# Key-value sums of a memory-attention block over 128 rows and eight array tiles instead of 96 rows and four

## Chip, cores and metric

One core of a Trainium2 chip runs the kernel. The metric is device time in microseconds (us), lower is better; quoted times are medians over several executions. The span of a profile (first to last instruction) is some 1.7 us shorter than the time of the same execution. All executions quoted here were fast (none was more than 1.5% above the fastest of its kernel). Tiles named `p_...` lie in PSUM, where TensorE writes, in banks; tiles named `t_...` lie in SBUF. A cited "Trainium skill" is a set of notes on the chip, named by page title.

## The reference

Eight batches, eight heads, 576 tokens, 64 columns a head. Keys and values are condensed into 32 memory rows a head with softmax weights from `phi`; queries attend to those rows; a gated feed-forward block follows.

```python
a = exp(phi - max(phi)); a = a / (sum(a, axis=2) + 1e-9)    # axis 2: the 576 tokens
k_m = einsum('bhsm,bhsd->bhmd', a, k)                       # (8, 8, 32, 64)
v_m = einsum('bhsm,bhsd->bhmd', a, v)
attn = softmax(q @ k_m.T / 8)                               # over 32 memory rows
x = (attn @ v_m) -> (4608, 512)                             # tokens x (heads * 64)
out = (silu(x @ w_gate) * (x @ w_val)) @ w_out              # d_ff 1536
```

## The kernel before

Tokens of a head lie on 96 partitions, six to a partition. The weighted sums over tokens (`p_kv`) are products of 96 rows by 32 columns: one array tile for each of four head pairs, both heads `g` of a pair in turn, all in one PSUM bank. VectorE divides by the denominators in one product of tensors each for keys and values. `NG` = 2, `NP` = 4, `J` = 6, `P` = 96, `D` = 64, `M` = 32.

```python
def kv_sum(b, p, parts):
    w0, w1 = parts[0], parts[-1] + 1
    n = (w1 - w0) * D
    for g in range(NG):
        for j in range(J):
            for i in range(NP):
                nc.tensor.matmul(p[32*i:32*i+32, n*g:n*(g+1)],
                    lhsT=ephis[b][:, j, g, i],
                    rhs=kvs[b][:, w0:w1, 2*i+g, j*D:(j+1)*D],
                    start=(j == 0), stop=(j == J-1), tile_position=(0, 32*i))

def run_sums():                        # batches 2 to 7
    o = NG * 2 * D
    p = bank([128, o + NG], FP32, "p_kv")
    kv_denominators(b, p, o)
    kv_sum(b, p, (0, 1))
    kv_reciprocal(b, p, o)
    kvv = p[:, 0:o].rearrange("p (g w d) -> p g w d", g=NG, w=2)
    k_norm(b, kvv[:, :, 0:1, :])       # one VectorE tensor_tensor
    v_norm(b, kvv[:, :, 1, :])         # one VectorE tensor_tensor
    done(p)
    if beside:
        beside()                       # the p_u products of another weight chunk
```

Batches 0 and 1 start while loads land. Their values are summed late and straight in transposed form, and dummy products (`p_warm`) fill TensorE:

```python
def v_direct(b):
    p = bank([128, NP, M], FP32, "p_vT")
    # ... 48 products of 96 rows x 64 columns ...
    nc.vector.tensor_copy(out=kTs[b][:, 2], in_=p.rearrange("p i m -> p (i m)"))

def warm(n):
    p = bank([128, DM], FP32, "p_warm")
    for _ in range(n):
        nc.tensor.matmul(p[:, 0:128], lhsT=bones, rhs=bones, start=True, stop=True)

warm(130)
# ... keys, queries, scores of batches 0 and 1, with smaller groups of dummies ...
v_direct(0)
nc.scalar.preload_act_table_set("silu_and_others")
norm(1, 0)                             # t_A of batch 1, VectorE
norm(1, 1)
warm(24)
v_direct(1)
warm(4)
run([u_half(0, (0,), 0, 0, "av"), u_half(1, (0,), 0, 0, "av")])   # first p_u group
warm(6)
for s in range(4):
    gv_gate(0, s)                      # first gate products
```

The softmax here doesn't subtract the row's maximum and nothing guards it: scores larger than these inputs give would overflow.

## Time and profile before

| | kernel before |
|---|---|
| time | 248.39 us (248.08 to 248.61, 3 runs) |
| TensorE busy | 239.5 us, 97% of a span of 246.6 us |
| VectorE / ScalarE busy | 157.9 us / 164.5 us |
| first denominators / first scores / first gate product | 11.10 / 14.89 / 28.21 us |

TensorE is the bound from about 28 us on.

### The profile page before, as it was taken

What the parts mean: (1) busy time and instruction counts of PE and PEld (TensorE: products, weight loads), DVE (VectorE), ACT (ScalarE), POOL (GpSimd) and SP (SyncE); (2) the same over time, 40 slices, a digit from 0 to 9 for tenths busy, and PEclk for the clock granted to TensorE, in tenths of its full rate; (3) what the DMA queues carried; (4) which work ended last, traced back from release to release, by engine and by line L of the source; (5) the groups of instructions that cost most, each with busy time, mean ns of one, the idle gap of its engine ahead of it and who ended that gap; (6) DMA issues with size and microseconds to landing.
All of it is one profiled execution on the core that took longest, in us unless ns stands there. A gap on an engine that the chain in (4) does not pass through costs nothing.

```text
span 246.6 us, 6607 instructions
## 1 busy us (share of the span) xinstructions
PE 239.5 (97%) x2600; PEld 151.2 (61%) x2600; DVE 157.9 (64%) x337; ACT 164.5 (67%) x356; POOL 51.4 (21%) x81
## 2 busy tenths in 40 slices
PE   7989999999999999999999999999999999999993
PEld 7965767774544766467646665476546655467543
DVE  0045599993338688478837778479746876587420
ACT  2447889885087577966896577866995678676201
POOL 8433432000060005071305230090007000000000
PEclk9999999999999999999999999999999999999998
DMA  6999999999699975995996499489414311310143
GB/s 182 206 203 203 199 207 205 232 207 184 143 158 243 247 174 82 216 297 112 153 246 177 80 152 242 136 123 187 94 44 120 69 43 43 88 43 0 45 129 85
DMA packets 47055, 37.00 MB, mean 150 GB/s; under 512 B 15920, under 2 KB 41776, under 8 KB 47024
## 3 DMA queue, kind: packets, MB, share of 16 engines
q0 software_dynamic: 25520, 22.42, 56.1%
q1 hardware_dynamic: 20496, 13.37, 22.5%
q10 hardware_dynamic: 1008, 0.79, 1.2%
q8 instruction: 20, 0.33, 0.5%
q14 instruction: 11, 0.09, 0.1%
HBM read 42.47 MB, written 9.44 MB: 210 GB/s over the span
## 4 chain that ended last, share of the span: by engine, by line
PE 95%; DVE 1%; ACT 1%; issue 0%
PE p_oo L512 38%; PE p_g L452 19%; PE p_v L452 19%; PE p_u L409 5%; PE p_warm L619 5%; PE p_kv L206 2%; PE p_oo L544 1%; DVE t_qT L348 1%; PE p_g L379 1%; PE p_g L358 1%; PE p_v L379 1%; PE p_vT L317 1%; ACT t_E L368 1%; PE p_T L270 0%; PE p_kv L226 0%
## 5 line engine op out<-in xcount | busy, mean ns | idle before, releaser
L512 PE MATMUL p_oo<-WO,t_h 128*128 128x512 bf16 x420 | 108.7, 380 | 0.0
L468 ACT ACTIVATE t_sg<-p_g 128x288 bf16<-128x288 f32 x192 | 76.3, 414 | 31.2 <-PE p_g L452 24.2
L475 DVE TENSOR_TENSOR t_h<-t_sg,p_v 128x288 bf16<-128x288 bf16 x192 | 83.4, 452 | 18.0 <-PE p_v L452 14.1
L452 PEld LDWEIGHTS <-t_U 128*128 128x128 bf16 x768 | 74.2, 98 | 30.7 <-issue 2.5
L452 PE MATMUL p_g<-t_A,t_U 128*128 128x288 bf16 x384 | 77.5, 286 | 0.1
L452 PE MATMUL p_v<-t_A,t_U 128*128 128x288 bf16 x384 | 76.9, 286 | 0.0
L512 PEld LDWEIGHTS <-t_h 128*128 128x128 bf16 x420 | 39.5, 98 | 41.1 <-issue 6.1
L524 DVE COPY t_o<-p_oo 128x512 f32<-128x512 f32 x27 | 18.6, 690 | 31.9 <-PE p_oo L512 29.4
L433 DVE CAST t_U<-p_u 128x512 bf16<-128x512 f32 x42 | 26.7, 683 | 6.8 <-PE p_u L409 6.8
L429 ACT CAST t_U<-p_u 128x512 bf16<-128x512 f32 x30 | 15.8, 592 | 8.9 <-PE p_u L409 8.9
L522 ACT COPY t_o<-p_oo 128x512 f32<-128x512 f32 x8 | 4.7, 588 | 20.1 <-PE p_oo L512 10.6
L115 POOL DMA_DIRECT2D t_q<-in_q_dram x6 | 4.7, 779 | 60.8 <-DMA t_qT<-t_q 59.5
L619 PE MATMUL p_warm<-bones 128*128 128x128 bf16 x198 | 15.2, 239 | 1.5 <-DVE bones L635 1.5
L176 ACT ACTIVATE t_ephi<-t_phi 96x768 bf16<-96x768 f32 x16 | 12.5, 843 | 4.2 <-DMA t_phi<-in_phi_dram 4.2
L409 PE MATMUL p_u<-W,t_kT 64*32 64x512 bf16 (+1 forms) x416 | 15.2, 365 | 0.1
L619 PEld LDWEIGHTS <-bones 128*128 128x128 bf16 x198 | 13.4, 109 | 2.2 <-DVE bones L635 1.5
L189 POOL COPY t_mark<-t_A 1x1 bf16<-1x1 bf16 x4 | 0.7, 180 | 54.9 <-DVE t_A L389 54.9
L368 ACT ACTIVATE t_E<-p_g 128x288 bf16<-128x288 f32 x16 | 6.6, 412 | 8.3 <-PE p_v L358 7.8
L389 DVE TENSOR_TENSOR t_A<-t_E,t_lz 128x576 bf16<-128x576 bf16 x16 | 11.5, 750 | 0.5 <-ACT t_lz L384 0.5
L384 ACT ACTIVATE t_lz<-t_lz 128x576 f32<-128x576 f32 x16 | 10.9, 683 | 0.5
L193 POOL TENSOR_TENSOR t_es<-t_es,t_ephi 96x256 f32<-96x256 f32 x16 | 10.7, 666 | 1.3
L610 ACT ACT_TABLE_LOAD x7 | 9.0, 1283 | 1.3 <-PEq L798 1.2
(58 smaller groups left out, 159.8 us busy)
## 6 DMA issues: line engine op xcount, KB each, us to landing
t_kv<-in_k_dram POOLq DMA_DIRECT2D x8, 576.0 KB, 9.6
t_kv<-in_v_dram POOLq DMA_DIRECT2D x8, 576.0 KB, 14.3
out_dram<-t_o SPq DMA_DIRECT2D x23, 192.0 KB, 2.5
t_phi<-in_phi_dram POOLq DMA_DIRECT2D x6, 576.0 KB, 16.5
t_q<-in_q_dram POOLq DMA_DIRECT2D x6, 576.0 KB, 8.0
out_dram<-t_o SPq DMA_DIRECT2D x24, 128.0 KB, 2.4
WO<-in_moe_w_out_dram POOLq DMA_DIRECT2D x3, 512.0 KB, 19.5
out_dram<-t_o SPq DMA_DIRECT2D x23, 64.0 KB, 2.1
```

The lines of the kernel that those rows point to most:

```text
L176: nc.scalar.activation(out=t[:, :, g].rearrange("p j i m -> p i j m"), in_=src[:, g], func=AF.Exp)
L384: nc.scalar.activation(out=lz, in_=lz, func=AF.Exp, scale=-1.0)
L389: nc.vector.tensor_tensor(out=a, in0=es.pop((b, g)), in1=lzs.pop((b, g)), op=ALU.mult)
L409: nc.tensor.matmul(p[g][32 * i:32 * i + 32, o:o + n], lhsT=kTs[b][64 * g:64 * g + 64, 2, 32 * i:32 * i + 32], rhs=w_part(w, c, i, g, halve ...
L429: nc.scalar.copy(out=t, in_=p)
L433: nc.vector.tensor_copy(out=t, in_=p)
L452: nc.tensor.matmul(p[:, 0:HALF], lhsT=Us[b, c, g][:, o // 2, which, 128 * (o % 2):128 * (o % 2 + 1)], rhs=atts[b, g][:, r], start=(g == 0) ...
L468: nc.scalar.activation(out=sg, in_=gate[:, 0:HALF], func=AF.Silu)
L475: nc.vector.tensor_tensor(out=dst, in0=sg, in1=val[:, 0:HALF], op=ALU.mult)
L512: nc.tensor.matmul(mine["p"], lhsT=hts[c, jf][:, 128 * u:128 * (u + 1)], rhs=WO[jf], start=(jf == 0), stop=(jf == NJF - 1),)
L524: nc.vector.tensor_copy(out=t_o, in_=mine["p"])
L619: nc.tensor.matmul(p[:, 0:128], lhsT=bones, rhs=bones, start=True, stop=True)
```

## The change

The intent: use all 128 partitions and both row halves of the array. Head pairs are laid over 128 partitions, 64 rows a head and nine tokens a row (`JK` = 9), so that a wave of sums is eight tiles of 64 x 32, two banks. Loads get fewer and longer pieces, and the sums have the tiling of `p_u`. Batches 0 and 1 have `phi` with zeros for the other head, so that products over 128 rows serve one head. Dummies become 512 columns wide. Cut to its core:

```diff
-        t = inp.tile([P, 2, H, J * D], BF16, tag="kv", name="t_kv")
-        nc.gpsimd.dma_start(out=t[:, 0], in_=k[b].rearrange("h (p j) d -> p h (j d)", p=P))
+        t = inp.tile([128, 2, NP, JK * D], BF16, tag="kv", name="t_kv")
+        nc.gpsimd.dma_start(out=t[:, 0], in_=head_pairs(k[b]))
 ...
-        for g in range(NG):
-            for j in range(J):
-                for i in range(NP):
+        for j in range(JK):
+            for i in range(NP):
+                for g in range(NG):
                     nc.tensor.matmul(
-                        p[32 * i:32 * i + 32, n * g:n * (g + 1)],
+                        p[g][32 * i:32 * i + 32, 0:n],
 ...
-                        tile_position=(0, 32 * i),
+                        tile_position=(64 * g, 32 * i),
 ...
+    def scaled_copy(out, p, r):
+        nc.vector.tensor_scalar(out=out, in0=p, scalar1=r, scalar2=None, op0=ALU.mult)
     def k_norm(b, p):                  # v_norm likewise
-        nc.vector.tensor_tensor(out=bk, in0=p..., in1=rSs[b]..., op=ALU.mult)
+        for g in range(NG):
+            scaled_copy(bk[:, g], x, rSs[b][:, g:g + 1])
 ...
     def v_direct(b):                   # 36 products of 128 rows
-        nc.vector.tensor_copy(out=kTs[b][:, 2], in_=p.rearrange("p i m -> p (i m)"))
+        for g in range(NG):
+            for o in range(2):
+                nc.vector.tensor_copy(
+                    out=dst[64 * g:64 * g + 64, :, o], in_=p[64 * o:64 * o + 64, :, g]
+                )
 ...
-    phi_exp(0)
-    phi_exp(1)
+    for b in range(2):
+        phi_zeros(b, nc.vector)
+        phi_exp_masked(b)
 ...
-    warm(130)                          # 130 products of 128 columns
+    warm(130, 0)                       # 32 of 512 columns and one of 256
```

More of the change, by code (lines that the diff above doesn't have):

```diff
@@ L40 @@
     P, J = 96, 6
+    JK = 9
     NG = 2
@@ L81, with head_pairs, load_phi @@
     Q_SLOT = (0, 1, 0, 0, 1, 0, 1, 0)
-    def load_phi(b, *engs):
-        t = inp.tile([P, H, J * M], FP32, tag="phi", name="t_phi")
-        n = H // len(engs)
-        for i, eng in enumerate(engs):
-            eng.dma_start(
-                out=t[:, n * i:n * (i + 1)],
-                in_=phi[b, n * i:n * (i + 1)].rearrange("h (p j) m -> p h (j m)", p=P),
-            )
+    def head_pairs(x):
+        return x.rearrange("h s d -> (h s d)").rearrange("(i p f) -> p i f", i=NP, p=128)
+    def load_phi(b, eng):
+        t = inp.tile([128, NP, JK * M], FP32, tag="phi", name="t_phi")
+        eng.dma_start(out=t, in_=head_pairs(phi[b]))
         phis[b] = t
     def load_k(b):
-        t = inp.tile([P, 2, H, J * D], BF16, tag="kv", name="t_kv")
-        nc.gpsimd.dma_start(out=t[:, 0], in_=k[b].rearrange("h (p j) d -> p h (j d)", p=P))
+        t = inp.tile([128, 2, NP, JK * D], BF16, tag="kv", name="t_kv")
+        nc.gpsimd.dma_start(out=t[:, 0], in_=head_pairs(k[b]))
         kvs[b] = t
     def load_v(b):
-        nc.gpsimd.dma_start(
-            out=kvs[b][:, 1], in_=v[b].rearrange("h (p j) d -> p h (j d)", p=P)
-        )
+        nc.gpsimd.dma_start(out=kvs[b][:, 1], in_=head_pairs(v[b]))
     def load_q_group(b, g):
@@ L167 @@
     ones1 = consts.tile([128, 1], BF16, tag="ones1", name="ones1")
+    ones2 = consts.tile([128, NG], BF16, tag="ones2", name="ones2")
     ephis, rSs, bks, bvs, kTs, es, atts = {}, {}, {}, {}, {}, {}, {}
     def phi_exp(b):
-        t = att.tile([P, J, NG, NP, M], BF16, tag="ephi", name="t_ephi")
-        src = phis.pop(b).rearrange("p (i g) (j m) -> p g i j m", g=NG, m=M)
+        t = att.tile([128, JK, NP, M], BF16, tag="ephi", name="t_ephi")
+        nc.scalar.activation(
+            out=t.rearrange("p j i m -> p i j m"),
+            in_=phis.pop(b).rearrange("p i (j m) -> p i j m", m=M),
+            func=AF.Exp,
+        )
+        ephis[b] = t
@@ L175, in phi_exp, with phi_exp_masked, phi_zeros @@
+    masked = {}
+    def phi_exp_masked(b):
+        t = masked[b]
+        src = phis.pop(b).rearrange("p i (j m) -> p i j m", m=M)
         for g in range(NG):
+            rows = slice(64 * g, 64 * g + 64)
             nc.scalar.activation(
-                out=t[:, :, g].rearrange("p j i m -> p i j m"), in_=src[:, g], func=AF.Exp
+                out=t[rows, :, g].rearrange("p j i m -> p i j m"), in_=src[rows], func=AF.Exp
             )
-        ephis[b] = t
+    def phi_zeros(b, eng):
+        t = att.tile([128, JK, NG, NP, M], BF16, tag=f"mphi{b}", bufs=1, name="t_mphi")
+        for g in range(NG):
+            eng.memset(t[64 * (1 - g):64 * (1 - g) + 64, :, g], 0.0)
+        masked[b] = t
@@ L181, with phi_of @@
+    def phi_of(b, g, j, i):
+        rows = slice(64 * g, 64 * g + 64)
+        return masked[b][rows, j, g, i] if b in masked else ephis[b][rows, j, i]
     esums = {}
     def phi_sum(b):
-        e = ephis[b].rearrange("p j g i m -> p j (g i m)")
+        e = ephis[b].rearrange("p j i m -> p j (i m)")
         mark = att.tile([1, 1], BF16, tag="mark", bufs=1, name="t_mark")
         nc.gpsimd.tensor_copy(out=mark, in_=atts[b - 1, 1][0:1, 0, 0:1])
-        t = att.tile([P, NG * 128], FP32, tag="es", bufs=1, name="t_es")
@@ L191, in phi_sum @@
-        nc.gpsimd.tensor_tensor(out=t, in0=e[:, 0], in1=e[:, 1], op=ALU.add)
-        for j in range(2, J):
-            nc.gpsimd.tensor_tensor(out=t, in0=t, in1=e[:, j], op=ALU.add)
-        hl = att.tile([P, 2, NG * 128], BF16, tag="ehl", bufs=1, name="t_ehl")
-        nc.gpsimd.tensor_copy(out=hl[:, 0], in_=t)
-        nc.gpsimd.tensor_tensor(out=hl[:, 1], in0=t, in1=hl[:, 0], op=ALU.subtract)
+        t = att.tile([128, 4, 128], FP32, tag="es", bufs=1, name="t_es")
+        add = lambda o, x, y: nc.gpsimd.tensor_tensor(out=o, in0=x, in1=y, op=ALU.add)
@@ L197, in phi_sum @@
+        add(t, e[:, 0:4], e[:, 4:8])
+        add(t[:, 0:2], t[:, 0:2], t[:, 2:4])
+        add(t[:, 0], t[:, 0], t[:, 1])
+        add(t[:, 0], t[:, 0], e[:, 8])
+        hl = att.tile([128, 2, 128], BF16, tag="ehl", bufs=1, name="t_ehl")
+        nc.gpsimd.tensor_copy(out=hl[:, 0], in_=t[:, 0])
+        nc.gpsimd.tensor_tensor(out=hl[:, 1], in0=t[:, 0], in1=hl[:, 0], op=ALU.subtract)
         esums[b] = hl
@@ L202, in kv_sum @@
         n = (w1 - w0) * D
-        for g in range(NG):
-            for j in range(J):
-                for i in range(NP):
+        for j in range(JK):
+            for i in range(NP):
+                for g in range(NG):
                     nc.tensor.matmul(
-                        p[32 * i:32 * i + 32, n * g:n * (g + 1)],
-                        lhsT=ephis[b][:, j, g, i],
-                        rhs=kvs[b][:, w0:w1, 2 * i + g, j * D:(j + 1) * D],
+                        p[g][32 * i:32 * i + 32, 0:n],
+                        lhsT=phi_of(b, g, j, i),
+                        rhs=kvs[b][64 * g:64 * g + 64, w0:w1, i, j * D:(j + 1) * D],
@@ L210, in kv_sum, with kv_denominators @@
                         start=(j == 0),
-                        stop=(j == J - 1),
-                        tile_position=(0, 32 * i),
-                    )
-    def kv_denominators(b, p, o):
+                        stop=(j == JK - 1),
+                        tile_position=(64 * g, 32 * i),
+                    )
+    def kv_denominators(b, p):
+        if b in masked:
+            for g in range(NG):
+                for j in range(JK):
+                    nc.tensor.matmul(
+                        p[:, g:g + 1],
+                        lhsT=masked[b][:, j, g].rearrange("p i m -> p (i m)"),
+                        rhs=ones1,
+                        start=(j == 0),
+                        stop=(j == JK - 1),
+                    )
+            return
@@ L216, in kv_denominators @@
         if b in esums:
             hl = esums.pop(b)
-            terms = [[hl[:, t, 128 * g:128 * (g + 1)] for t in range(2)] for g in range(NG)]
+            terms = [hl[:, t] for t in range(2)]
         else:
-            terms = [
-                [ephis[b][:, j, g].rearrange("p i m -> p (i m)") for j in range(J)]
-                for g in range(NG)
-            ]
-        for g in range(NG):
-            for n, x in enumerate(terms[g]):
-                nc.tensor.matmul(
-                    p[:, o + g:o + g + 1],
-                    lhsT=x,
-                    rhs=ones1[0:P, :],
-                    start=(n == 0),
-                    stop=(n == len(terms[g]) - 1),
-                )
@@ L234, in kv_reciprocal @@
-    def kv_reciprocal(b, p, o):
-        r = att.tile([128, NG, 1, 1], FP32, tag="rS", name="t_rS")
-        nc.vector.reciprocal(
-            out=r.rearrange("p g a c -> p (g a c)"), in_=p[:, o:o + NG]
-        )
+            terms = [ephis[b][:, j].rearrange("p i m -> p (i m)") for j in range(JK)]
+        for n, x in enumerate(terms):
+            nc.tensor.matmul(p, lhsT=x, rhs=ones2, start=(n == 0), stop=(n == len(terms) - 1))
+    def kv_reciprocal(b, p):
+        r = att.tile([128, NG], FP32, tag="rS", name="t_rS")
+        nc.vector.reciprocal(out=r, in_=p)
@@ L239, in kv_reciprocal @@
         rSs[b] = r
+    def scaled_copy(out, p, r):
+        nc.vector.tensor_scalar(out=out, in0=p, scalar1=r, scalar2=None, op0=ALU.mult)
     def k_norm(b, p):
         bk = att.tile([128, NG, 2, D], BF16, tag="bk", name="t_bk")
-        nc.vector.tensor_tensor(
-            out=bk,
-            in0=p.to_broadcast([128, NG, 2, D]),
-            in1=rSs[b].to_broadcast([128, NG, 2, D]),
-            op=ALU.mult,
-        )
+        for g in range(NG):
+            x = p[g][:, 0:D].rearrange("p (a d) -> p a d", a=1).to_broadcast([128, 2, D])
+            scaled_copy(bk[:, g], x, rSs[b][:, g:g + 1])
@@ L252, in v_norm @@
         bv = att.tile([128, NG, D], BF16, tag="bv", name="t_bv")
-        nc.vector.tensor_tensor(
-            out=bv,
-            in0=p,
-            in1=rSs[b].rearrange("p g a c -> p g (a c)").to_broadcast([128, NG, D]),
-            op=ALU.mult,
-        )
+        for g in range(NG):
+            scaled_copy(bv[:, g], p[g][:, D:2 * D], rSs[b][:, g:g + 1])
         bvs[b] = bv
@@ L278, in run_sums @@
         def run_sums():
-            o = NG * 2 * D
-            p = bank([128, o + NG], FP32, "p_kv")
-            kv_denominators(b, p, o)
+            o = 2 * D
+            p = [bank([128, CH], FP32, f"p_kv{g}") for g in range(NG)]
+            kv_denominators(b, p[0][:, o:o + NG])
             kv_sum(b, p, (0, 1))
-            kv_reciprocal(b, p, o)
-            kvv = p[:, 0:o].rearrange("p (g w d) -> p g w d", g=NG, w=2)
-            k_norm(b, kvv[:, :, 0:1, :])
-            v_norm(b, kvv[:, :, 1, :])
-            done(p)
+            kv_reciprocal(b, p[0][:, o:o + NG])
+            k_norm(b, p)
+            v_norm(b, p)
+            done(*p)
             if beside:
@@ L297, in denominators @@
             p = bank([128, NG], FP32, "p_S")
-            kv_denominators(b, p, 0)
-            kv_reciprocal(b, p, 0)
+            kv_denominators(b, p)
+            kv_reciprocal(b, p)
             done(p)
         def sums():
-            p = bank([128, NG * D], FP32, "p_kv")
+            p = [bank([128, D], FP32, f"p_kv{g}") for g in range(NG)]
             kv_sum(b, p, (0,))
-            k_norm(b, p.rearrange("p (g a d) -> p g a d", g=NG, a=1))
-            done(p)
+            k_norm(b, p)
+            done(*p)
         return [denominators, sums, lambda: kv_T(b, (0,))]
     def v_direct(b):
-        p = bank([128, NP, M], FP32, "p_vT")
-        for i in range(NP):
-            for j in range(J):
-                for g in range(NG):
+        p = bank([128, NP // 2, NG, M], FP32, "p_vT")
+        for n in range(NP // 2):
+            for j in range(JK):
+                for o in range(2):
                     nc.tensor.matmul(
-                        p[64 * g:64 * g + 64, i],
-                        lhsT=kvs[b][:, 1, 2 * i + g, j * D:(j + 1) * D],
-                        rhs=ephis[b][:, j, g, i],
+                        p[64 * o:64 * o + 64, n],
+                        lhsT=kvs[b][:, 1, 2 * n + o, j * D:(j + 1) * D],
+                        rhs=masked[b][:, j, :, 2 * n + o],
                         start=(j == 0),
-                        stop=(j == J - 1),
-                        tile_position=(0, 64 * g),
-                    )
-        nc.vector.tensor_copy(out=kTs[b][:, 2], in_=p.rearrange("p i m -> p (i m)"))
+                        stop=(j == JK - 1),
+                        tile_position=(0, 64 * o),
+                    )
+        dst = kTs[b][:, 2].rearrange("p (n o m) -> p n o m", n=NP // 2, o=2)
+        for g in range(NG):
+            for o in range(2):
+                nc.vector.tensor_copy(
+                    out=dst[64 * g:64 * g + 64, :, o], in_=p[64 * o:64 * o + 64, :, g]
+                )
         done(p)
@@ L424, in u_round @@
                 src = p[g][:, 0:(w1 - w0) * n].rearrange("p (a f) -> p a f", f=HC)
-                banks.append((dst, src, p[g], rSs[b][:, g, 0] if b in scaled else None))
+                banks.append((dst, src, p[g], rSs[b][:, g:g + 1] if b in scaled else None))
         for (t, p, home, r), e in zip(banks, evac):
@@ L613, in gv_slots, with warm @@
         return [lambda s=s: gv_slot(b, s) for s in range(2 * NJF)]
-    def warm(n):
+    def warm(n, narrow=0):
         p = bank([128, DM], FP32, "p_warm")
-        for _ in range(n):
-            nc.tensor.matmul(p[:, 0:128], lhsT=bones, rhs=bones, start=True, stop=True)
+        x = bones.rearrange("p (a c) -> p a c", a=1)
+        sizes = [1] * narrow + [4] * ((n - narrow) // 4)
+        sizes += [n - sum(sizes)] if n > sum(sizes) else []
+        for a in sizes:
+            nc.tensor.matmul(
+                p[:, 0:128 * a],
+                lhsT=bones,
+                rhs=x.to_broadcast([128, a, 128]) if a > 1 else bones,
+                start=True,
+                stop=True,
+            )
         free.insert(0, held.pop(id(p))[0])
@@ L633 @@
     nc.vector.memset(ones1, 1.0)
+    nc.vector.memset(ones2, 0.0)
+    for g in range(NG):
+        nc.vector.memset(ones2[64 * g:64 * g + 64, g:g + 1], 1.0)
     for h in range(4):
```

## The prediction

> **What bounds the kernel now.** I read the page of the kernel before first, then its waits of PE, then the timelines of PE, DVE and POOL around one key-value sum, and the start.
>
> ```profile
> PE 239.5 (97%) x2600; PEld 151.2 (61%) x2600; DVE 157.9 (64%) x337; ACT 164.5 (67%) x356; POOL 51.4 (21%) x81
> ...
> PE 95%; DVE 1%; ACT 1%; issue 0%
> ```
> ```profile
> PE p_warm L619 <- DVE bones L635: 1.5, 1, 1.5
> PE p_g L379 <- ACT t_E L368: 0.4, 1, 0.4
> PE p_g L358 <- DVE t_qT L348: 0.2, 1, 0.2
> PE p_T L270 <- PE p_warm L619: 0.2, 1, 0.2
> ```
> The first fence is the busy time of the engines and the head of the chain that ended last; the second is every wait of PE (total us, times, longest). PE works 97% of the span, is 95% of the chain, and waits 2.3 us in all, every wait within the first 22 us. From about 28 us to the end, a nanosecond off PE is a nanosecond off the kernel, as long as nothing else starts to wait. Before 28 us it is different: dummy products fill PE while loads land, so PE is busy there without being the bound.
>
> The part that the change rewrites, batch 4's sums, in the timeline of PE and of DVE (start us, duration us, engine, line):
> ```profile
> 111.10 0.24 PE L226 MATMUL p_kv<-ones,t_ehl 96*128 96x1 bf16 x4
> 111.27 0.85 PE L206 MATMUL p_kv<-t_kv,t_ephi 96*32 96x128 bf16 x48
> 112.06 0.63 PE L409 MATMUL p_u<-W,t_kT 64*32 64x512 bf16 x16
> 112.62 0.60 PE L512 MATMUL p_oo<-WO,t_h 128*128 128x512 bf16 x2
> ```
> ```profile
> 112.18 0.17 DVE L236 RECIPROCAL t_rS<-p_kv 128x2 f32<-128x2 f32 x1 [0.36 <-PE p_kv L206]
> 112.39 0.42 DVE L243 TENSOR_TENSOR t_bk<-p_kv,t_rS 128x256 bf16<-128x256 f32 x1
> 112.73 0.28 DVE L253 TENSOR_TENSOR t_bv<-p_kv,t_rS 128x128 bf16<-128x128 f32 x1
> 112.93 1.28 DVE L433 CAST t_U<-p_u 128x512 bf16<-128x512 f32 x2
> ```
> Durations overlap, so I take differences of starts. The sums hold PE from 111.27 to 112.06, 0.79 us. The records of single instructions show four products (one per column tile) starting within some 10 ns, and the next four 56 ns after them: 12 waves of 56 ns are 0.67 us. The other 0.11 us appear only where the next product uses another tiling: 149 ns from the last product to the next instead of 56, so about 93 ns for the change of tiling.
>
> The start, from the timelines of PE and POOL:
> ```profile
> 23.54 0.94 PE L317 MATMUL p_vT<-t_ephi,t_kv 96*64 96x32 bf16 x48
> 24.41 1.51 PE L619 MATMUL p_warm<-bones 128*128 128x128 bf16 x24
> 25.98 0.94 PE L317 MATMUL p_vT<-t_ephi,t_kv 96*64 96x32 bf16 x48
> ```
> ```profile
> 26.10 0.74 POOL L142 DMA_DIRECT2D W<-in_moe_w_val_dram  x1 [2.58 <-DMA t_kv<-in_v_dram]
> ```
> POOL's next issue waited for the values of batch 1, landed at 25.8 by the DMA records; PE's second direct value product starts at 25.98, after 24 dummies. The dummies are tuned to the loads.
>
> **What the Trainium skill says.** "TensorE: Matmul & The Clock Gate", section "Wait — 56ns, not 53.3ns?", gives starts N/2.4 GHz + about 2.5 ns apart once warm, N/1.2 GHz cold, and a floor near 25 ns. The trace agrees: 56 ns at 128 columns, 215.8 at 512, 25.1 to 25.5 at one column, 106.7 cold (until 5.96 us). "TensorEngine Tiling (Array Packing)", "Key Properties", says that changing the tiling mode drains TensorE; the 93 ns agree. Its "Gotcha 1: PSUM Pressure" wants different banks for different row tiles, which is why the new sums take two banks where one served; the kernel before already does so in its p_u products. "DMA: Bandwidth & Descriptors", "Why small descriptors are slow", names a fixed cost per descriptor. Here it is small: the quickest DMA engine finished loads of 768 pieces of 768 B every 2.90 us, of 512 pieces of 512 B every 1.34, and of 512 pieces of 1024 B every 2.54. Per engine (a sixteenth of the pieces) that is 0.0734 ns a byte plus 4.3 ns a piece.
>
> **The change part by part.**
>
> *Sums of batches 2 to 7.* 48 products in 12 waves of four become 72 in 9 waves of eight: 3 x 56 = 0.168 us less a batch. This supposes that eight tiles stream as freely as four. Line L409 runs the same eight tiles at 256 columns at 107 ns a wave, which is the bare 256/2.4. The doubt is supply: in the 64-column sums at 17.5 us the last pairs of weight load and product come 8.3 ns apart, against 7 ns (56/8) needed here. But about 36 pairs had gone faster before that, from a filled queue; 36 + 504/8.3 = 97 pairs are on hand in the time that 72 take, so I charge nothing.
>
> *Tiling changes.* In batches 3 to 7 the sums are followed by p_u, which has the same tiling after the change: 0.093 us less in each of five.
>
> *Denominators.* Batches 4 to 7 do two products instead of four, 2 x 25 = 0.050 us each. Batches 2 and 3 do 9 instead of 12, 0.076 each.
>
> Sum on PE: 6 x 0.168 + 5 x 0.093 + 4 x 0.050 + 2 x 0.076 = 1.83 us, all on the bound.
>
> *Normalising on DVE.* Two products of tensors (0.42 and 0.28, together 0.62) become four scalings of 128 columns. L435 scalings take 743 ns at 512 columns and 478 at 256, so 345 at 128; neighbours overlap by some 86, so 4 x 345 - 3 x 86 = 1.12 us, 0.5 more. Counted from the last sum product, DVE starts the reciprocal at +0.27 and lets go of the first bank (after its value scaling) at +1.36. PE meanwhile does p_u (0.56), two p_oo (0.43 and a 0.09 tiling change), one gate (0.24), and then wants that bank at about +1.30 for p_v. With the semaphore that is a wait of about 0.1 us, in five batches 0.5 us given back. The later banks are in time by 0.2 us or more by the same count.
>
> *ACT and POOL.* One exponential of 1152 columns (about 1.18 us, from 843 ns at 768 and 0.9 ns a column in the t_E and t_lz rows) instead of two of 768 (1.6): off the path. POOL's sum for the denominators covers 512+256+128+128 columns instead of five times 256 at 666 ns, so about 1 us sooner: no wait to remove.
>
> *Loads.* A k or v load is 512 pieces of 1152 B: 32 x (4.3 + 84.6) = 2.84 us instead of 2.90. With phi, values of batch 1 land some 0.3 us sooner. No wait after 28 us is one for a load, so this counts only at the start.
>
> *The start.* Three small memsets ahead of the diagonal blocks delay the first dummy by about 0.3 us. The 130 dummies as 32 of 512 and one of 256 run at 54 ns a 128 columns instead of 55.6 when warm; with the same clock edge they end some 0.2 us sooner. Batch 0's and 1's denominators are 18 products instead of 12: +0.17 each after the rest of the pipeline. The 64-column sums are held by supply, 0.33 against 0.36 us. Key scaling is +0.19 on the path to the transpose at 12.73. So I see the middle of the start about 0.3 later. The direct value product has 18 waves instead of 24 at 32 ns (the two 64-column weight loads seem to set it): -0.18 each; the dummies between give 0.06. But its copy on DVE is four of 64 columns, some 0.64 us instead of 0.29, and PE's p_u at 27.3 waits for that. Together +0.1 us, with perhaps 0.4 either way. The zeros (four memsets on DVE between 2 and 7 us) and the masked exponentials (6.6 to 11.1 us on ACT, batch 0's half done by 9) are in time for PE at 10.9.
>
> Total: -1.83 + 0.5 + 0.1 = -1.2 us: 247.1 us.
>
> **The rivals.** (a) *Supply of instructions bounds eight tiles.* For it: 8.3 ns a pair in the 64-column sums, and 50% more pairs. Then 72 x 8.3 = 0.60 us and a batch saves 0.07 instead of 0.17; the total is about 247.8. Against it: the filled queue. (b) *The second bank and longer DVE work become waits.* One bank more is held, and DVE is already 64% busy. If the p_u copies and the products of gate and value are late too, 0.3 us a batch is lost and the whole gain goes: 248.4. Against it: the counted slack, and a DVE that idles 14 us waiting for p_v alone. (c) *The start is freed.* If phi and keys land so much sooner, or in step on all 16 engines (the last engine is now up to 1.9 us behind the first), that PE gets to p_u sooner, 0.5 us more is won: 246.3. Against it: PE there hangs on copies by DVE and exponentials by ACT, not on loads alone. (d) *DVE scalings from PSUM cost less than extrapolated*, so no wait at all: 246.6.
>
> **Range and chances.** (c) and (d) set the low end, (a) and a mild (b) the high one, and three runs of the kernel before already spread over 0.5 us. I take 246.0 to 248.2. A gain over 2% would need 5 us, more than all the time of the rewritten products; a loss over 2% would need a new wait of 1 us in every batch. So 3% faster, 96% the same, 1% slower.
>
> **What would show it right or wrong.** In the changed profile: sums of 72 products with 0.50 to 0.56 us from their first start to that of p_u (0.60 or more says rival a); no tiling gap before p_u; PE still above 96% busy; a row of PE waiting for DVE's t_bv or t_bk of 0.1 us, five times (0.3 or more says b; none says d); the first p_u within 0.4 us of 27.3 (much earlier says c). I am wrong outright if PE gains waits on loads or on p_u copies after 28 us, or if the p_oo or gate products change their spacing.

## More of the kernel before

The prediction shows the page, the waits and one batch's sums. What it does not show is the end of the start; this is the timeline of the kernel before (start us, duration us, engine, line, operation, then idle time and its releaser in brackets):

```profile
25.95 0.76 DVE L389 TENSOR_TENSOR t_A<-t_E,t_lz 128x576 bf16<-128x576 bf16 x1 [0.47 <-ACT t_lz L384]
...
26.95 0.29 DVE L325 CAST t_kT<-p_vT 128x128 bf16<-128x128 f32 x1 [0.25 <-PE p_vT L317]
...
27.30 0.41 PE L409 MATMUL p_u<-W,t_kT 64*32 64x256 bf16 x16
...
28.21 0.77 PE L452 MATMUL p_g<-t_A,t_U 128*128 128x288 bf16 x5
```

VectorE is free for 0.25 us before the one copy behind the direct value product. The copy is done at 27.24, and the 16 `p_u` products follow in one go.

## The result, and the profile after

After: 248.82 us median (248.48 to 249.47, 4 runs) beside 248.28 us (248.08 to 248.61) for the kernel before. A ratio here is the mean time of one kernel's fast runs over that of the other's of the same rounds, so not quite the ratio of the quoted medians: 1.0024, 95% interval 1.0000 to 1.0047. Later the same kernel gave 0.9998 (0.9984 to 1.0013). The time stayed; the predicted 247.1 us and its range to 248.2 us missed it.

The page of the kernel after (busy us and share of each engine; head of the chain that ended last), then the waits of its TensorE (total us, times, longest us):

```profile
PE 236.3 (96%) x2594; PEld 143.0 (58%) x2621; DVE 163.0 (66%) x364; ACT 164.1 (66%) x350; POOL 47.5 (19%) x77
...
PE 87%; DMA 4%; DVE 4%; issue 2%; ACT 2%; SPq 0%; DVEq 0%
```
```profile
PE p_oo L538 <- issue: 2.7, 17, 0.2
PE p_warm L649 <- DVE bones L672: 1.7, 1, 1.7
PE p_g L405 <- ACT t_E L394: 0.3, 1, 0.3
PE p_u L435 <- DVE t_kT L349: 0.2, 1, 0.2
```

The trace has 2621 weight loads but 2594 products, so 27 records of products are missing, and the first row of waits (17 of 0.2 us before output products) is most likely just those holes: in e1, which has records of both output products behind the sums of batch 4, there is none. Row four is real and new.

Two stretches of the trace tell where the time went. From the first denominators (`p_S`) to the first gate product the kernel after takes 17.95 us, before 17.11. From there to the last output product's start it takes 213.88 us, before 214.35. So +0.84 us at the start and -0.47 us in the middle; with +0.02 us ahead of both, the last product starts 0.39 us later.

The middle, batch 4: the timeline of TensorE and that of VectorE of the kernel after.

```profile
111.98 0.19 PE L261 MATMUL p_kv<-ones,t_ehl 128*128 128x2 bf16 x2
112.10 0.80 PE L233 MATMUL p_kv<-t_kv,t_ephi 64*32 64x128 bf16 x72
112.69 0.66 PE L435 MATMUL p_u<-W,t_kT 64*32 64x512 bf16 x16
113.51 0.38 PE L538 MATMUL p_oo<-WO,t_h 128*128 128x512 bf16 x1 [0.16 <-issue]
113.72 0.41 PE L478 MATMUL p_g<-t_A,t_U 128*128 128x288 bf16 x2
114.15 0.42 PE L478 MATMUL p_v<-t_A,t_U 128*128 128x288 bf16 x2
```
```profile
113.09 0.17 DVE L265 RECIPROCAL t_rS<-p_kv 128x2 f32<-128x2 f32 x1 [0.38 <-PE p_u L435]
113.29 0.61 DVE L269 TENSOR_SCALAR t_bk<-p_kv,t_rS 128x128 bf16<-128x128 f32 x2
113.82 0.47 DVE L269 TENSOR_SCALAR t_bv<-p_kv,t_rS 128x64 bf16<-128x64 f32 x2
114.20 1.28 DVE L459 CAST t_U<-p_u 128x512 bf16<-128x512 f32 x2
```

The sums now hold TensorE for 0.59 us (112.10 to 112.69), not 0.79. The tiling gap is gone: the records of single products show 8 ns between the last sum and the first `p_u`. But `p_v` starts 0.43 us after `p_g`, where 0.245 is normal: it starts 0.06 us after VectorE's first value scaling, the third of the four, which ends at 114.09 and is the last reader of the first bank. (0.13 us of this comes from a late start: VectorE's reciprocal began 0.405 us after the last sum here, and 0.27 in this kernel's other batches.) The single records also show how the 72 pairs of weight load and product go: the first 32 in 56 ns waves, a hole of some 50 ns, then 40 of them 8.33 ns apart, and the first eight `p_u` products keep that step.

The start, from the timelines of the kernel after:

```profile
26.23 0.76 PE L338 MATMUL p_vT<-t_mphi,t_kv 128*64 128x64 bf16 x36
...
27.27 0.96 DVE L349 CAST t_kT<-p_vT 64x64 bf16<-64x64 f32 x4
27.36 0.45 PE L435 MATMUL p_u<-W,t_kT 64*32 64x256 bf16 x9
...
28.03 0.55 PE L435 MATMUL p_u<-W,t_kT 64*32 64x256 bf16 x7 [0.21 <-DVE t_kT L349]
28.27 0.88 DVE L461 TENSOR_SCALAR t_U<-p_u,t_rS 128x256 bf16<-128x256 f32 x2
...
29.07 0.40 PE L478 MATMUL p_g<-t_A,t_U 128*128 128x288 bf16 x2
```

The first `p_u` is only 0.06 us later than before, but the group is broken in two: its second half (batch 1's) follows the four copies, and the last five products start after the fourth. The span from the group's first to last start grew from 0.14 to 0.94 us, and the first gate product is 0.86 us later than before.

A caution for such readings: the moment at which TensorE's clock rises to full speed differed from execution to execution, from 4.4 to 7.5 us over all profiles here, and the dummies carry half of that into everything after them. "TensorE: Matmul & The Clock Gate", "Part 1: The HAM clock gate", of the Trainium skill says that the deciding window of 3.4 us runs free of the kernel's start; the spread of 3.1 us agrees. I therefore compare stretches, not points. The first stretch repeats to 0.01 us for the same start where TensorE waits for no load in it. The last one does not: the same middle took from 213.80 us (e10) to 214.73 (e9), so one profile alone does not fix it to better than that. This table has them (us, from the records of the profiled executions):

| kernel | clock rises | first `p_S` | `p_S` to first gate | first gate to last `p_oo` |
|---|---|---|---|---|
| before | 5.96 | 11.10 | 17.11 | 214.35 |
| after | 6.10 | 11.12 | 17.95 | 213.88 |
| e1: old start, new middle | 6.63 | 11.42 | 17.10 | 213.88 |
| e2: new start, old middle | 4.87 | 10.51 | 17.94 | 214.35 |
| e3: scalings by bank | 5.92 | 11.03 | 17.94 | 213.64 |
| e9: after, again | 4.46 | 10.31 | 17.94 | 214.73 |
| e13: one copy | 5.58 | 10.87 | 17.16 | 214.43 |
| e12: tuned | 6.57 | 10.05 | 17.59 | 213.66 |

### The profile page after: what moved, and what is told of

The parts are those of the page before. It is cut to its first block, busy times and chain, and to the rows that moved or that the text cites. A ratio compares the mean times of both kernels' runs of the same rounds, so it can differ in the third digit from the quotient of the medians.

```text
span 247.1 us, 6641 instructions
## 1 busy us (share of the span) xinstructions
PE 236.3 (96%) x2594; PEld 143.0 (58%) x2621; DVE 163.0 (66%) x364; ACT 164.1 (66%) x350; POOL 47.5 (19%) x77
## 4 chain that ended last, share of the span: by engine, by line
PE 87%; DMA 4%; DVE 4%; issue 2%; ACT 2%; SPq 0%; DVEq 0%
PE p_oo L538 32%; PE p_g L478 20%; PE p_v L478 19%; PE p_u L435 5%; PE p_warm L649 4%; DMA out_dram<-t_o 4%; PE p_kv L233 2%; DVE t_qT L374 1%; PE p_g L405 1%; DVE t_A L415 1%; PE p_g L384 1%; PE p_v L405 1%; DVE t_kT L349 1%; ACT t_E L394 1%; DVE t_o L550 1%
## 5 line engine op out<-in xcount | busy, mean ns | idle before, releaser
L538 PE MATMUL p_oo<-WO,t_h 128*128 128x512 bf16 x393 | 101.8, 379 | 3.0 <-issue 2.7
L494 ACT ACTIVATE t_sg<-p_g 128x288 bf16<-128x288 f32 x192 | 76.5, 414 | 34.0 <-PE p_g L478 27.3
L501 DVE TENSOR_TENSOR t_h<-t_sg,p_v 128x288 bf16<-128x288 bf16 x192 | 82.4, 452 | 17.0 <-PE p_v L478 12.6
L649 PE MATMUL p_warm<-bones 128*128 128x512 bf16 (+2 forms) x53 | 14.9, 415 | 1.7 <-DVE bones L672 1.7
L435 PE MATMUL p_u<-W,t_kT 64*32 64x512 bf16 (+1 forms) x416 | 16.0, 365 | 0.3 <-DVE t_kT L349 0.2
L649 PEld LDWEIGHTS <-bones 128*128 128x128 bf16 x53 | 5.3, 108 | 8.1 <-issue 3.0
L461 DVE TENSOR_SCALAR t_U<-p_u,t_rS 128x512 bf16<-128x512 f32 (+1 forms) x14 | 8.8, 669 | 1.4 <-PE p_u L435 1.4
L435 PEld LDWEIGHTS <-t_kT 64*32 64x32 bf16 x416 | 4.9, 89 | 8.2 <-issue 6.7
```

Of the source, the lines that this page charges most:

```text
L435: nc.tensor.matmul(p[g][32 * i:32 * i + 32, o:o + n], lhsT=kTs[b][64 * g:64 * g + 64, 2, 32 * i:32 * i + 32], rhs=w_part(w, c, i, g, halve ...
L494: nc.scalar.activation(out=sg, in_=gate[:, 0:HALF], func=AF.Silu)
L501: nc.vector.tensor_tensor(out=dst, in0=sg, in1=val[:, 0:HALF], op=ALU.mult)
L538: nc.tensor.matmul(mine["p"], lhsT=hts[c, jf][:, 128 * u:128 * (u + 1)], rhs=WO[jf], start=(jf == 0), stop=(jf == NJF - 1),)
L649: nc.tensor.matmul(p[:, 0:128 * a], lhsT=bones, rhs=x.to_broadcast([128, a, 128]) if a > 1 else bones, start=True, stop=True,)
```

## Experiments

Each ran in five rounds beside the kernel before. Kernels are compared only within the same rounds.

**e1 and e2: one half of the change each.** Both layouts are kept in the code, and a set says which batches use the old one; e1 also has the old dummies and the old order of the start.

```diff
+    OLD = (0, 1)                   # e1;  e2: OLD = (2, 3, 4, 5, 6, 7)
```

> Batches 0 and 1 as in the kernel before (96 rows, one bank, dummies of 128 columns), batches 2 to 7 as in the changed kernel. Theory S (the profile of the changed kernel is 0.86 us behind by the gate at 29 us and wins 0.47 us back later): 0.4 to 0.6 us faster than before, about 247.8 us, and the first gate at 28.2 us. Rival M (the new sums win nothing, their waits eat all): within 0.1 us of before.

> The reverse: batches 0 and 1 as in the changed kernel, 2 to 7 as before. Theory S: 0.8 to 0.9 us slower than before, about 249.1 us, all of it by 29 us. Rival M: no slower than the changed kernel, 248.8 us or less.

Measured: e1 248.12 us, ratio 0.9971 (0.9956 to 0.9985); e2 249.42 us, ratio 1.0020 (1.0002 to 1.0038). In these four profiles the stretches fall apart cleanly: the start takes 17.10 or 17.94 us and the middle 213.88 or 214.35 us, according to the half that was changed. That the two new middles agree to 0.01 us is chance: in e1 batch 4 had no late reciprocal, but the sums of batch 6 took 0.14 us longer. So the new middle alone is a gain of some 0.5 us in the trace (0.7 in time; the interval, 0.4 to 1.1, holds both), and the new start alone a loss of 0.84 (0.5 in time, interval 0.05 to 0.95).

**e15: half the columns in the sums of batches 2 to 7.** Is it streaming or supply that holds the 72 pairs? (The result is wrong.)

```diff
-            kv_sum(b, p, (0, 1))
+            kv_sum(b, p, (0,))
```

> The changed kernel with the sums of batches 2 to 7 over the 64 columns of k alone (v's half left out, k's sums scaled twice, so the result is wrong on purpose); the same 72 pairs of weight load and product. Supply theory: a wave streams 27 ns instead of 53, and yet from the first sum to p_u in batch 4 the time falls only from 0.586 to about 0.55 us, and the kernel by 0.0 to 0.3 us in all. Streaming theory (nine waves at N/2.4 GHz set it): 0.586 falls to about 0.33 us, and the kernel by 1.0 to 1.5 us, unless p_v's wait for VectorE takes part of it back.

Measured: 248.99 us, ratio 1.0001 (0.9979 to 1.0023). The timeline of TensorE in e15:

```profile
111.74 0.75 PE L233 MATMUL p_kv<-t_kv,t_ephi 64*32 64x64 bf16 x72
112.30 0.66 PE L435 MATMUL p_u<-W,t_kT 64*32 64x512 bf16 x16
```

Half the streaming took the sums from 0.586 to 0.559 us, no further. After the first 32 pairs and a hole, pairs come 8.33 ns apart whether they stream 64 or 128 columns. Nor is it the weight loads as such: in the first burst of e15, 31 of them start within 0.10 us, 3.3 ns apart. So streaming is ruled out, and supply is what is left; the traces do not show the supply itself.

**e6: the sums cut in two around half of `p_u`.** If pairs come from a queue, eight products of 512 columns should let it fill.

```diff
+            kv_sum(b, p, (0, 1), range(4))        # 32 pairs
+            beside(0)                             # 8 p_u products
-            kv_sum(b, p, (0, 1))
+            kv_sum(b, p, (0, 1), range(4, 9))     # 40 pairs
```

> The changed kernel with the sums of batches 3 to 7 cut in two: 32 pairs (weight load and product), then the eight products of 512 columns that used to follow the sums (first half of p_u), then the other 40 pairs. Theory (pairs on eight tiles run at 56 ns a wave as long as instructions are queued ahead, 32 pairs' worth; after that each pair costs 8.33 ns of supply whatever its columns; eight products of 512 columns take some 0.21 us in which the queue fills again): from the first sum to the first output product after p_u falls from 1.19 us to 0.95 to 1.05 us in batch 4, so 0.15 to 0.25 us in each of five batches; the pairs after the p_u run at 7 ns, not 8.33, for at least the first 17 of them. Some of it can be given back where transposed values wait for VectorE, since the scalings then start later in relation to p_u. Time 0.5 to 1.0 us under the changed kernel's. Rival (8.33 ns is what a product with its weights takes on these tiles once a burst is over, not supply): the second 40 pairs take 8.33 ns each as well, and the time stays within 0.2 us.

Measured: 250.13 us, ratio 1.0055 (1.0035 to 1.0075): slower, against the theory's gain. The timeline of TensorE in e6:

```profile
111.59 0.42 PE L233 MATMUL p_kv<-t_kv,t_ephi 64*32 64x128 bf16 x32
111.84 0.44 PE L438 MATMUL p_u<-W,t_kT 64*32 64x512 bf16 x8
112.06 0.57 PE L233 MATMUL p_kv<-t_kv,t_ephi 64*32 64x128 bf16 x40
112.41 0.44 PE L438 MATMUL p_u<-W,t_kT 64*32 64x512 bf16 x8
...
113.23 0.41 PE L481 MATMUL p_g<-t_A,t_U 128*128 128x288 bf16 x2
113.74 0.42 PE L481 MATMUL p_v<-t_A,t_U 128*128 128x288 bf16 x2
```

The second piece's first 24 pairs started within 180 ns, some of them 4 ns apart, so 8.33 ns is not what a pair needs on these tiles. But then the step of 8.33 ns came back with new holes, and the 40 pairs took 0.355 us to the next `p_u`, no better than in one piece. Worse, the sums now end 0.24 us later after their start (0.82 instead of 0.58), and VectorE's chain begins at their end: `p_v` comes 1.33 us after the last sum. In batches 5 to 7 each loses 0.23 us. How the queue fills while products wait remains open.

**e3: scalings ordered by bank.** Keys and values of bank 0 first, so that it is free after two scalings.

```diff
-            k_norm(b, p)
-            v_norm(b, p)
+            for g in range(NG):
+                scaled_copy(bk[:, g], x, r)
+                scaled_copy(bv[:, g], p[g][:, D:2 * D], r)
```

> The changed kernel with the four scalings on DVE ordered by bank (key and value of the first bank, then of the second), so that the first bank comes free after two of them. If the gap of 0.18 us before p_v after the sums is the wait for that bank: it falls to 0.05 or less, and the kernel gains 0.3 to 0.5 us over the changed one (about 248.4 us). Rival (the gap is the supply of instructions, or the bank wait only moves to the next one): gain under 0.1 us.

Measured: 248.50 us, ratio 0.9987 (0.9971 to 1.0002). VectorE's and then TensorE's timeline in e3, batch 4:

```profile
113.15 0.35 DVE L269 TENSOR_SCALAR t_bk<-p_kv,t_rS 128x128 bf16<-128x128 f32 x1
113.42 0.28 DVE L269 TENSOR_SCALAR t_bv<-p_kv,t_rS 128x64 bf16<-128x64 f32 x1
```
```profile
113.72 0.41 PE L483 MATMUL p_g<-t_A,t_U 128*128 128x288 bf16 x2
113.96 0.41 PE L483 MATMUL p_v<-t_A,t_U 128*128 128x288 bf16 x2
```

The first `p_v` follows `p_g` by 0.24 us again in all five batches, and the stretch of the middle is 0.24 us shorter; 0.3 to 0.5 was expected. Not all of it is the order's: of the 0.19 us in batch 4, 0.13 is the late reciprocal, which did not fall there in e3; in batches 5 to 7 it gains about 0.05 each. In batch 3 it gains nothing, because there the products wait for other banks next (see below). The waits for the first bank are real, and small.

**e13: one copy behind the direct value product.** (The values lie wrong; the result is wrong.)

```diff
-        for g in range(NG):
-            for o in range(2):
-                nc.vector.tensor_copy(
-                    out=dst[64 * g:64 * g + 64, :, o], in_=p[64 * o:64 * o + 64, :, g]
-                )
+        nc.vector.tensor_copy(out=kTs[b][:, 2], in_=p.rearrange("p n g m -> p (n g m)"))
```

> The changed kernel with one copy of 128 columns on VectorE in place of the four of 64 behind each direct value product; the values then lie in the wrong places, so the result is wrong on purpose. Theory (those copies, after the normalisation that precedes them, hold the second half of the first p_u group): from the first denominators to the first gate product 17.2 us in place of 17.94, the span of that p_u group back at 0.14 to 0.25 us from 0.94, the time 0.5 to 0.8 us under the changed kernel's. Rival (the normalisation before the copies holds p_u whatever their number): 17.6 us or more.

Measured: 248.50 us, ratio 0.9985 (0.9967 to 1.0003). The timeline of TensorE in e13:

```profile
27.12 0.41 PE L431 MATMUL p_u<-W,t_kT 64*32 64x256 bf16 x16
27.47 0.50 PE L645 MATMUL p_warm<-bones 128*128 128x512 bf16 x2
28.02 1.15 PE L474 MATMUL p_g<-t_A,t_U 128*128 128x288 bf16 x8
```

The `p_u` group is whole again, and the start takes 17.16 us: of its 0.84 us, 0.79 hang on the number of copies. In the time less of it arrived: this execution lost 0.4 us again at 79 us (see e9).

**e5: the second normalisation of batch 1 behind the copies.**

```diff
     norm(1, 0)
-    norm(1, 1)
     warm(24)
     v_direct(1)
+    norm(1, 1)
```

> The changed kernel with one line moved: the second normalisation of batch 1's weights (t_A, 752 ns on VectorE at 26.49 to 27.24 us of its trace) comes after the four copies of the direct value product instead of before them. Theory (the four copies begin only at 27.27 because that instruction stands before them, and the second p_u group waits for the fourth): copies begin about 26.9 to 27.0, the p_u group's span falls from 0.94 to about 0.65 us, and the time falls 0.2 to 0.3 us against the changed kernel's (ratio to the kernel before about 1.001). But t_A is needed by batch 1's first gate products soon after; if those wait instead, the gain is nil. Rival (the copies are not on the path; TensorE is held by something else in that stretch, such as the weights' landing): p_u group moves by less than 0.1 us and the time stays.

Measured: 249.06 us, ratio 1.0019 (1.0002 to 1.0037). TensorE in e5:

```profile
26.51 0.97 PE L435 MATMUL p_u<-W,t_kT 64*32 64x256 bf16 x16
...
27.97 0.28 PE L478 MATMUL p_g<-t_A,t_U 128*128 128x288 bf16 x1
28.50 0.66 PE L478 MATMUL p_g<-t_A,t_U 128*128 128x288 bf16 x4 [0.25 <-DVE t_U L461]
```

The first gate came 0.24 us sooner after `p_S` (17.70), but the product after it started 0.53 us later, where 0.12 is usual, because the moved instruction now stood before `t_U` on VectorE. The gain was given back, as the expectation allowed.

**e8, e4 and e14: the dummies.** e8 is the kernel before with wide dummies; e4 and e14 are the kernel after with narrow ones, in all groups and in the first alone.

```diff
-    warm(130, 0)
+    warm(130, 130)                 # e14; e4: narrow = n in every group
```

> The kernel before with dummies of 512 columns only, nothing else of the change. In the changed kernel narrow dummies cost 2 us (1.5 us in which TensorE waited for nothing the profile shows, beside a fetch of instructions at 12.1 us). Theory 1 (wide dummies are neutral where no fetch of instructions is late; the kernel before's profile shows no such stall): 248.2 to 248.8, same within 0.2 us. Theory 2 (the stall also falls on some of the kernel before's runs, or its fetch costs a little): faster by 0.3 to 1 us. Theory 3 (wide dummies hold TensorE past the moment at which the work is ready): slower by 0.1 to 0.4 us.

> The changed kernel with dummies of 128 columns, as before. Theory: the width of the dummies is neutral, as their end was 11.1 us in both profiles: within 0.2 us of the changed kernel. Rival (wide dummies delay the start, by more time to the next product or by a later clock edge): 0.4 us or more faster than the changed kernel.

> The changed kernel with dummies of 128 columns in the first group only (130 of them in place of 33), wide ones in all the others. Theory (each instruction ahead of a fixed point brings the first fetch of instructions forward, to 12 us and earlier, where the queues are full; a narrow first group alone moves it by 97 instructions, nearly all of the difference): the stall of over 1 us appears again near 12 to 15 us, and the time is 250 us or more. Rival (the stall needs narrow dummies in the later groups, where TensorE has a few spare cycles only): no stall, time as the changed kernel's within 0.3 us.

Measured: e8 248.86 us, ratio 1.0010 (0.9997 to 1.0023); e4 250.88 us, 1.0076 (1.0053 to 1.0098); e14 250.02 us, 1.0040 (1.0018 to 1.0063). In the kernel before, the width is neutral. In the kernel after it is not, which neither expectation of e4 had foreseen: beside its own ratio of 1.0024 and 0.9998, narrow dummies cost 0.5 to 0.8% in e4 and 0.2 to 0.4% in e14. They were run at other times. From the waits of TensorE in e4 and in e14:

```profile
PE p_warm L649 <- issue: 1.5, 1, 1.5
```
```profile
PE p_T L293 <- DVE t_bk L269: 1.0, 1, 1.0
```

In e4 TensorE stood still from 12.9 to 14.45 us with no releaser. In e14 its next product started at 14.50, although `t_bk`, to which the wait is put down, was done at 13.65; 0.85 us are unexplained. In both the first packet (16 KB) on the instruction queue moved at 12.1 us, while loads kept the DMA engines busy; in the kernel after it moved at 15.3. In e4 the halt was followed by 6.8 us at half clock. The kernel before has such a packet at 11.0 us, e1, e7 and e11 (narrow dummies too) between 10.6 and 11.8, and none of them halts there. And e12, with wide dummies and the packet at 15.5, stands still for 0.5 us at 17.3 (below). So a late fetch of instructions is a possible cause, not a shown one, and narrow dummies are not the whole of it.

**e9, e10 and e11: fewer dummies.** The loads land sooner in the new layout: values of batch 1 by 0.9 us on the quickest DMA engine and by 1.5 on the slowest (complete at 24.3 us, before at 25.8). Does the start use that? e9 is the kernel after, unchanged; e10 and e11 are after and before with 24 dummies less.

```diff
-    warm(130, 0)
+    warm(106, 0)                   # e11: warm(106)
```

> The changed kernel as it is, as a control for the other three on the same chip. 248.3 to 249.2 us, ratio to the kernel before 0.999 to 1.004. In its profile the stretch from the first denominators to the first gate product takes 17.94 us, as in all five profiles of this start so far (17.10 in the kernel before's), and the rest to the last output product is 0.4 to 0.5 us shorter than the kernel before's.

> The changed kernel with 24 fewer dummies (106 for 130 columns blocks of 128) ahead of the first denominators, nothing else. Theory (the change brings the loads of batches 0 and 1 and of the expert weights in 1.0 to 1.1 us sooner, but TensorE does not use it: the dummies hold it, and what follows is its own and VectorE's work, 0.84 us longer than before; so the start has some 1.9 us of room against the landings): everything from the first denominators on moves 1.2 us forward and stays there; the time falls 0.9 to 1.3 us, to 247.2 to 247.9. Rival (loads or the exponentials bound this start): the first denominators wait for phi or the sums for keys, or the direct value products for v, and the time falls by less than 0.4 us. A third way: with fewer dummies the clock's rise comes late and the start is slower.

> The kernel before with 106 dummies for 130, nothing else. Theory (there the landings bind: v of batch 1 landed at 25.8 us and its product started at 26.0, weights landed within 0.1 us of need in two other profiles that started early): at most 0.3 us faster, the 1.2 us being lost in waits for loads between 12 and 36 us of the profile. Rival (loads do not bind there either): 0.9 to 1.3 us faster.

Measured: e9 248.66 us, ratio 0.9998; e10 248.06 us, 0.9971 (0.9956 to 0.9986); e11 248.76 us, 1.0007 (0.9993 to 1.0022). The timeline of TensorE in e11, then that of VectorE in e9:

```profile
27.14 0.62 PE L409 MATMUL p_u<-W,t_kT 64*32 64x256 bf16 x16 [0.58 <-DMA W<-in_moe_w_gate_dram]
```
```profile
76.34 0.69 DVE L550 COPY t_o<-p_oo 128x512 f32<-128x512 f32 x1 [4.17 <-DMA out_dram<-t_o]
76.95 1.42 DVE L415 TENSOR_TENSOR t_A<-t_E,t_lz 128x576 bf16<-128x576 bf16 x2
```

With the old layout an earlier start only waits for the expert weights, so it is bound by landings at 27 us. With the new layout there is no such wait, and 24 dummies less are worth 0.27% or some 0.7 us beside e9. This is less than the expected 0.9 to 1.3: an early start can be lost again later. e9 shows how. It reached the first gate 0.82 us sooner than the first profile of the same kernel, thanks to its clock, and lost 0.7 us of that at 79 us, where VectorE's output copy had waited for an output transfer and `t_A` and the gates stood behind it. So its middle was 0.38 us longer than that of the kernel before, not 0.4 to 0.5 shorter as expected.

**e7 and e12: put together.** e7 is e1 with e3's order and e6's cut; e12 is the kernel after with e3's order, 106 dummies, and

```diff
     norm(1, 0)
-    norm(1, 1)
-    warm(24)
+    warm(16)
     v_direct(1)
     warm(4)
     run([u_half(0, (0,), 0, 0, "av"), u_half(1, (0,), 0, 0, "av")])
+    norm(1, 1)
```

> Batches 0 and 1 as in the kernel before (with its dummies of 128 columns), batches 2 to 7 as in the changed kernel, scalings ordered by bank, sums cut in two around half of p_u. If the three effects add: 248.1 (old start, new middle) less 0.3 (bank order) less 0.5 to 1.0 (cut): 246.8 to 247.4, ratio to the kernel before 0.991 to 0.995. If supply is not the limit: 247.8, ratio 0.997.

> The changed kernel with 106 dummies, 16 in place of 24 between the two direct value products, the second normalisation of batch 1's weights behind the first evacuations of p_u, and the scalings ordered by bank. If the reasons found so far hold: 1.2 us from the dummies, 0.3 to 0.5 from the two others at the start (the 0.93 us span of the first p_u group falls to 0.4 or less), 0.3 from the bank order: 246.6 to 247.3, ratio 0.992 to 0.996. If the start is bound by loads: 248.0.

Measured: e7 248.34 us, ratio 0.9992 (0.9981 to 1.0004). The cut does not pay: in batches 3 to 7 the first `p_v` starts 1.89 us after the first sum, in e3, without the cut, 1.86. And in its profile the old start waited 0.5 us for the values of batch 1, so it does not test the sum of the three effects cleanly. e12 247.19 us (246.65 to 247.47), ratio 0.9941 (0.9928 to 0.9954), with a correct result. TensorE in e12:

```profile
26.18 0.98 PE L440 MATMUL p_u<-W,t_kT 64*32 64x256 bf16 x16
27.09 0.50 PE L654 MATMUL p_warm<-bones 128*128 128x512 bf16 x2
27.65 0.53 PE L483 MATMUL p_g<-t_A,t_U 128*128 128x288 bf16 x3
```

The copies still stretch the `p_u` group, so the expected 0.4 us for it was wrong; but everything comes earlier, and no load is waited for. This profile has the halt of 0.5 us named above, within the sums of batch 1, with no releaser.

## Why the prediction was wrong

It expected a time within 2% of before, which held, but 1.2 us less, and the time stayed. Two terms of its sum were far off, the sums' supply and the copies at the start.

1. **The sums: "36 + 504/8.3 = 97 pairs are on hand ... so I charge nothing" failed.** The doubt was named and argued away. The working counts on supply going on while the first pairs drain. In the records there is a hole after the 32nd pair, and the 33rd starts 0.253 us after the first, hardly sooner than if all had come 8.33 ns apart (32 x 8.33 = 0.267): the head start is given back. From there on a pair costs 8.33 ns (e15). So the sums and the tiling change give 0.20 us in batch 4 instead of 0.168 + 0.093 = 0.26, and the 16 `p_u` pairs behind them lose 0.03 more (0.559 to 0.590 us to the first output product, by e1 and e3, which have its record), which the prediction did not think of. Its own test read 0.59 us, between its "0.50 to 0.56" and rival (a)'s "0.60 or more"; e15 decides for (a).
2. **The tiling changes and the denominators held.** The gap before `p_u` is 8 ns; the two denominators of batch 4 take 0.053 us less, predicted 0.050.
3. **The wait for VectorE was right in kind, too small in sum, and not in the place.** Predicted: 0.1 us for the first bank in five batches, the later banks in time "by 0.2 us or more". Measured: about 0.05 in batches 5 to 7, 0.18 in batch 4 (0.13 of it the late reciprocal), and 0.3 in batch 3. There 0.26 us are later banks: VectorE's two copies of `p_u` end at 88.41 and 89.01 us, and the next products start 0.05 us after each. That is a wait for `p_u` copies after 28 us, which the prediction had named as a sign of being wrong outright. Batch 2 loses another 0.08 before its transposes. In sum some 0.7 us against 0.5. The page's waits list none of this; it is read from the starts of single records. Rival (b) in full (0.3 us in every batch) did not happen. So of 1.83 us on TensorE some 1.2 came, 0.7 went, and the middle gained 0.47 us, where 1.33 was expected.
4. **The start: "Together +0.1 us" was +0.84.** The term that failed is the copy, "some 0.64 us instead of 0.29". Four copies took 0.96 us (starts 245 ns apart), and they began at 27.27 instead of 26.95, because the batch's second `t_A` stood before them on VectorE. That instruction had moved with everything in the middle of the start, 0.48 us later at the first scores: two times 0.15 for denominators (0.17 predicted), and 64-column sums that grew from 0.36 to 0.55 us, where "0.33 against 0.36" was predicted. Here the prediction did not use its own rate: 24 pairs more at 8.3 ns on the 0.35 us before make 0.55. TensorE won its share back in the shorter direct value product (0.19 us each, predicted 0.18) and the shorter dummies, so the first `p_u` came within 0.06 us of before; the sign that the prediction had chosen, within 0.4 us of 27.3, held and did not see the broken group. VectorE did not win it back. e13 puts 0.79 of the 0.84 us on the copies.
5. **Rival (c), a freed start, was half right.** Loads landed 0.9 to 1.5 us sooner, not 0.3, but nothing used it, because dummies and VectorE set the start. e10 and e12 use it.

What stays open: how the instruction queue is refilled (e6), and what halts TensorE at the start (e4, e14, e12).

## What to carry to other kernels

Count instructions as well as columns: when many small tiles take turns, pairs of weight load and product set the pace, and a wave that is cheaper to stream need not be cheaper. Follow every delay on the second engine too: TensorE had caught up by the first `p_u`, but the delayed VectorE instruction in front of the copies had not. And when a change makes loads land sooner, move the fillers that were tuned to the old landing, or the gain is not used.

## What the Trainium skill lacked or had wrong

- "TensorE: Matmul & The Clock Gate", "Architectural detail: the array is 16× 32×32, not 1× 128×128", gives TensorE a queue of 64 instructions; the 32 pairs (64 instructions) that go fast here agree. No page that I found says at what step pairs on several tiles come after that: on eight tiles of 64 x 32 it was 8.33 ns, after a hole of 50 to 100 ns, for products of 64, 128 and 512 columns alike. It holds 72 pairs to 0.55 to 0.59 us.
- "TensorEngine Tiling (Array Packing)", "Key Properties", says that a change of tiling drains TensorE, without a size: it was about 93 ns here.
- No page that I found says that TensorE can halt at the start with nothing to wait for: 1.5 us in e4 and 0.85 us in e14, both near 13 us and after the first instruction packet at 12.1 us, and 0.5 us in e12 at 17.3. The cause is not shown.
